# An attention and GEGLU block: last two chunks of 256 queries, Gelu table in the tail, PV in groups of four, LN1 partly on Pool

One core of one Trainium2 chip. The metric is the device time of one execution in microseconds, lower is better. A run is one execution; the first of each kernel is also profiled. PE is TensorE, PEld its weight loads, DVE VectorE, ACT ScalarE, POOL GpSimd, SP SyncE.

## The reference

```
x: [1, 2048, 640]   wqkv: [640, 1920]   wo: [640, 640]     32 heads of 20
w_gate, w_up: [640, 1728]   w_down: [1728, 640]            all bf16, LayerNorm without weights

h  = x + softmax(q k^T * 20**-0.5) v @ wo     with q, k, v = layernorm(x) @ wqkv
out = h + (gelu_tanh(layernorm(h) @ w_gate) * (layernorm(h) @ w_up)) @ w_down
```

## The kernel before

The program lists operations with their reads, writes, PSUM banks and a guessed duration. A small list scheduler, run when the program is built, turns these into one fixed order for each engine.

The queries go in four chunks of 512. In chunk 0 attention shares TensorE with the projections. In the later chunks it shares TensorE with the "post" stage of the chunk before it: output projection, second LayerNorm, gate/up, down. The post stage of the last chunk comes after all attention, with nothing beside it: the tail.

A head has 20 dimensions, so four heads fit in four 32-row groups of the array for QK, and in four 32-column groups for PV. In chunk 0 a unit is two score tiles (two banks), in later chunks three.

```python
tiles = [(c, g, kt, j) for c in range(NC) for g in range(NG) for kt in range(NT) for j in range(4)]
n2 = 64 * NG
units = [tiles[i:i + 2] for i in range(0, n2, 2)] + [tiles[i:i + 3] for i in range(n2, len(tiles), 3)]

def unit(u):
    ...                                                    # (cut: QK matmuls, one group of 2 or 3)
    op("act", I("activation", pts[:, u % 3, 0:n], PS[...], ACT.Exp, scale=SCALE), ...)
    for i, (c, g, kt, j) in enumerate(tl):                 # PV, right after its own exp
        op("pe", I("matmul", PS[32 * j:32 * j + VW, 512 * 6:512 * 7], v_all[:, kt, 4 * g + j, :], pts[...],
                   tile_position=(0, 32 * j), ...), 0.13, P_PV, ...)

for i in range(4):                                         # LN1, four tiles of 128 rows at a time
    for t in range(4 * i, 4 * i + 4):
        ln_stats(x_sb[:, t, :], t, ...)                    # DVE
    ln_rsqrt(4 * i, P_BG)                                  # DVE, 17 small operations on [128, 4]
    for t in range(4 * i, 4 * i + 4):
        ln_apply(x_sb[:, t, :], t, ...)                    # DVE tensor_scalar (x - mu) * rs, 128x640
        transposes(...)                                    # PE, evacuated by ACT

def post(c, banks):                                        # gate/up part of it
    for f in range(NF):                                    # 14 blocks of hidden units
        ...                                                # gate matmuls into a bank
        # DVE: copy, square, multiply-add;  ACT: Tanh;  DVE: multiply-add
        ...                                                # up matmuls
        # DVE: (tanh chain) * 0.5 * up
```

Pool pads the q and k weights in the prologue (12 copies); before that it fills memory with zeros. The post stages beside attention have one PSUM bank, number 7; the tail has all eight.

## Time and profile before

1160.09 us, median of three runs (1157.93 to 1163.11). Stages, read off the timeline of the profiled run (1161.9 us):

| stage | from, to (us) | length | bound by |
|---|---|---|---|
| prologue, to the first exp | 0, 51.1 | 51.1 | DVE queue, then projections |
| chunk 0, to the first 1536-column exp | 51.1, 341.2 | 290.2 | TensorE |
| chunks 1 to 3, to the end of the last exp | 341.2, 1064.5 | 723.3 | ScalarE |
| tail | 1064.5, 1161.9 | 97.4 | DVE in gate/up |

The table of windows of the kernel before at these times. Each line has the stretch, its length, and the busy microseconds of each engine (with its instruction count), then the granted TensorE clock, the share of the DMA engines and GB/s:

```profile
core 0: us, PE busy (x) PEld busy (x) DVE busy (x) ACT busy (x) POOL busy (x), PEclk, DMA share, GB/s
0.00:51.06 51.06, 27.09 (x182) 13.95 (x183) 41.60 (x160) 15.07 (x22) 19.31 (x37) 1.00 0.36 122
51.06:341.23 290.17, 283.98 (x1496) 85.66 (x1495) 122.90 (x228) 246.35 (x256) 0.00 (x0) 1.00 0.00 1
341.23:1064.50 723.27, 639.20 (x4162) 183.09 (x4160) 225.80 (x456) 711.90 (x554) 0.00 (x0) 0.90 0.05 15
1064.50:1161.90 97.40, 66.44 (x339) 32.54 (x339) 62.88 (x130) 8.81 (x15) 0.00 (x0) 0.89 0.03 11
```

Read across each line for the engine that is nearly as busy as the stretch is long. In chunk 0 that is PE (284 of 290), in chunks 1 to 3 ACT (712 of 723), in the tail neither: PE and DVE take turns. A busy PE is not PE at its peak, since matmuls overlap and their ends are modelled; the 639 us of chunks 1 to 3 hold the post stages of chunks 0 to 2 as well.

Two lines of the groups by shape of the kernel before, the only two copies of Pool; the columns are line, engine, operation, names, shapes, count, then busy us and mean ns of one, then idle before it:

```profile
L257 POOL COPY regw<-rege 128x560 bf16<-128x560 bf16 x10 | 6.6, 662 | 0.6
L257 POOL COPY regw<-rege 128x400 bf16<-128x400 bf16 x2 | 1.1, 534 | 0.2
```

Besides these, Pool sets memory and builds two identity masks of 128x128.

The timeline of PE in chunk 0 of the kernel before (start, duration, group, count). The end of a matmul is modelled, so read start to start:

```profile
122.38 0.39 PE L257 MATMUL ps<-qt_all,kt_all 32*128 32x512 bf16 x2
122.70 0.39 PE L257 MATMUL ps<-pts,v_all 128*21 128x512 bf16 x2
123.02 0.45 PE L477 MATMUL ps<-regw 128*128 128x320 bf16 x2
123.40 0.39 PE L257 MATMUL ps<-qt_all,kt_all 32*128 32x512 bf16 x2
```

QK to PV is 0.32 us and PV to the projections is 0.32 us, for two matmuls each. In a later chunk of the same trace, QK to PV is 0.32 us for three:

```profile
440.63 0.39 PE L257 MATMUL ps<-qt_all,kt_all 32*128 32x512 bf16 x3 [0.17 <-ACT pts L257]
440.95 0.39 PE L257 MATMUL ps<-pts,v_all 128*21 128x512 bf16 x3
```

### The profile page before, as it was taken

The numbers are of one execution on the slowest core, as the hardware profiler recorded it, in microseconds if no ns is written. First come the engines' busy times: TensorE is split into PE (matmuls) and PEld (weight loads), VectorE is DVE, ScalarE is ACT, GpSimd is POOL, SyncE is SP. The second block draws the span as 40 slices with busy tenths as digits, with TensorE's granted clock in tenths as the row PEclk, the third lists the DMA queues.
The fourth block names the chain that finished last, engine by engine and source line by source line (L and its number), as shares of the span: only waits on it lengthen the run. The fifth ranks groups of instructions, "written<-read, shape, count | busy, mean of one in ns | idle before, by whom it ended". The sixth has DMA issues, their size and how long they took to land.

```text
span 1161.9 us, 14374 instructions
## 1 busy us (share of the span) xinstructions
PE 1016.7 (88%) x6176; PEld 315.2 (27%) x6176; DVE 453.2 (39%) x973; ACT 982.1 (85%) x846; POOL 19.3 (2%) x37
## 2 busy tenths in 40 slices
PE   2999999999998988988898888998989888888567
PEld 1332332222222222222122222222222222322224
DVE  7733335535634444411024444210143444112783
ACT  1598887797699999999999999999999999996010
POOL 6000000000000000000000000000000000000000
PEclk9999999999999899999567999988598999995899
DMA  5000000000014000000000000000000000000000
GB/s 203 12 1 1 1 1 1 1 1 1 1 69 173 1 1 1 1 12 24 1 12 1 1 1 1 7 6 23 1 12 1 1 1 1 12 18 7 11 0 23
DMA packets 11823, 18.69 MB, mean 16 GB/s; under 512 B 688, under 2 KB 9840, under 8 KB 11760
## 3 DMA queue, kind: packets, MB, share of 16 engines
q1 hardware_dynamic: 11760, 17.78, 4.5%
q8 instruction: 48, 0.79, 0.3%
q14 instruction: 15, 0.12, 0.0%
HBM read 15.16 MB, written 2.62 MB: 15 GB/s over the span
## 4 chain that ended last, share of the span: by engine, by line
ACT 56%; PE 33%; DVE 9%; DMA 1%; issue 1%; SPq 0%; DVEq 0%
ACT pts L257 54%; PE ps L257 18%; PE ps L477 7%; ACT rege L257 2%; PE ps L676 2%; DVE rege L257 2%; PE ps L512 1%; PE ps L643 1%; DVE stats L257 1%; PE ps L443 1%; PE ps L661 1%; DMA rege<-in_A_x_dram 1%; DVE rege L648 1%; PE ps L612 1%; PE ps L588 1%
## 5 line engine op out<-in xcount | busy, mean ns | idle before, releaser
L257 ACT ACTIVATE pts<-ps 128x1536 bf16<-128x1536 f32 (+1 forms) x768 | 951.6, 1474 | 59.5 <-PE ps L257 58.4
L257 PE MATMUL ps<-qt_all,kt_all 32*128 32x512 bf16 x2048 | 318.0, 416 | 81.7 <-ACT pts L257 64.4
L257 PE MATMUL ps<-pts,v_all 128*21 128x512 bf16 x2048 | 324.6, 418 | 0.9 <-ACT pts L257 0.9
L257 PEld LDWEIGHTS ps<-qt_all,kt_all 32*128 32x128 bf16 x2048 | 73.8, 92 | 331.4 <-ACT pts L257 258.4
L477 PE MATMUL ps<-regw 128*128 128x512 bf16 (+1 forms) x480 | 136.6, 359 | 1.9 <-DVE v_all L539 0.6
L257 PEld LDWEIGHTS ps<-pts,v_all 128*21 128x21 bf16 x2048 | 72.7, 89 | 197.6 <-issue 187.6
L257 ACT ACTIVATE rege<-rege 128x512 f32<-128x512 bf16 (+1 forms) x56 | 46.7, 835 | 66.7 <-DVE rege L257 66.7
L661 PE MATMUL ps<-rege,regw 128*128 128x512 bf16 (+1 forms) x280 | 79.3, 388 | 19.6 <-ACT rege L257 17.7
L676 PE MATMUL ps<-regw,rege 128*128 128x320 bf16 x448 | 85.6, 305 | 1.1 <-DVE rege L665 1.0
L643 PE MATMUL ps<-rege,regw 128*128 128x512 bf16 (+1 forms) x280 | 85.4, 401 | 1.1 <-DVE rege L451 0.6
L257 DVE SCALAR_TENSOR_TENSOR rege<-rege 128x512 bf16<-128x512 bf16 (+1 forms) x112 | 76.5, 688 | 17.0 <-ACT rege L257 14.6
L648 DVE CAST rege<-ps 128x512 bf16<-128x512 f32 (+1 forms) x56 | 38.5, 688 | 82.3 <-PE ps L643 82.0
L680 DVE TENSOR_TENSOR rege<-ps,rege 128x320 bf16<-128x320 f32 x32 | 15.7, 491 | 137.5 <-PE ps L676 137.5
L665 DVE SCALAR_TENSOR_TENSOR rege<-rege,ps 128x512 bf16<-128x512 bf16 (+1 forms) x56 | 38.3, 684 | 64.1 <-PE ps L661 64.1
L257 DVE COPY osb<-ps 128x512 f32<-128x512 f32 x32 | 22.1, 690 | 104.1 <-PE ps L257 103.8
L477 PEld LDWEIGHTS ps<-regw 128*128 128x128 bf16 x480 | 40.8, 98 | 69.4 <-issue 48.5
L676 PEld LDWEIGHTS ps<-regw,rege 128*128 128x128 bf16 x448 | 34.9, 97 | 43.1 <-issue 28.6
L443 PE MATMUL ps<-ident,xn_t 128*128 128x128 bf16 x160 | 18.6, 272 | 29.3 <-DVE xn_t L257 29.0
L501 DVE TENSOR_SCALAR kt_all<-ps,e 128x512 bf16<-128x512 f32 x28 | 21.0, 749 | 57.2 <-PE ps L477 57.2
L661 PEld LDWEIGHTS ps<-rege,regw 128*128 128x128 bf16 (+1 forms) x280 | 20.5, 99 | 59.1 <-ACT rege L257 24.6
L504 DVE CAST qt_all<-ps 128x512 bf16<-128x512 f32 x31 | 21.2, 685 | 38.1 <-PE ps L477 38.1
L477 PE MATMUL ps<-wo,rege 128*128 128x320 bf16 x160 | 33.8, 329 | 0.5 <-DVE rege L624 0.4
(57 smaller groups left out, 417.0 us busy)
## 6 DMA issues: line engine op xcount, KB each, us to landing
rege<-in_A_x_dram SPq DMA_DIRECT2D x4, 640.0 KB, 10.1
rege<-in_A_x_dram SPq DMA_DIRECT2D x16, 160.0 KB, 2.2
out_dram<-rege SPq DMA_DIRECT2D x16, 160.0 KB, 1.8
regw<-in_B_w_gate_dram SPq DMA_DIRECT2D x1, 2160.0 KB, 8.2
regw<-in_B_w_up_dram SPq DMA_DIRECT2D x1, 2160.0 KB, 13.2
regw<-in_B_w_down_dram SPq DMA_DIRECT2D x1, 2080.0 KB, 19.5
rege<-in_A_wqkv_dram SPq DMA_DIRECT2D x1, 1600.0 KB, 8.2
regw<-in_A_wqkv_dram SPq DMA_DIRECT2D x1, 800.0 KB, 11.2
```

Of the source, the lines that this page charges most:

```text
L257: return lambda eng: getattr(eng, method)(*args, **kwargs)
L443: op("pe", lambda eng, a=a: eng.transpose(bank16(bk, D)[:, 128 * a:128 * a + 128], src[:, a * 128:(a + 1) * 128], ident[:]), c_mm(128), pr ...
L477: yield op("pe", lambda eng, l=l, r=r, k=k: eng.matmul(bank(bk, n), l, r, start=(k == 0), stop=(k == len(steps) - 1)), c_mm(n), prio, read ...
L501: op("dve", lambda eng: eng.tensor_scalar(dst, bank(bk), e0[:, 0:1], None, ALU.add), c_dve(512), prio, reads=[key, "e0"], writes=[(nm, g, ...
L504: op("dve", lambda eng: eng.tensor_copy(dst, bank(bk)), c_dve(512), prio, reads=[key], writes=[(nm, g, c)], rel=[bk])
L512: op("pe", lambda eng: eng.matmul(bank(b2), gm[:], sq[:, sqi, :], start=True, stop=True), c_mm(512), prio, reads=[("sq", sqi), "gq", "gqh" ...
L643: op("pe", lambda eng, a=a, bg=bg, f=f, m=m: eng.matmul(bank(bg)[0:m, :], wg[:, a, f * 128:f * 128 + m], hnT[:, a, :], start=(a == 0), sto ...
L648: op("dve", lambda eng, bg=bg, g16=g16, m=m: eng.tensor_copy(g16, bank(bg)[0:m, :]), c_dve(512), p, reads=[kg], writes=[("gb", i)], rel=[b ...
L661: op("pe", lambda eng, a=a, bu=bu, f=f, m=m: eng.matmul(bank(bu)[0:m, :], wu[:, a, f * 128:f * 128 + m], hnT[:, a, :], start=(a == 0), sto ...
L665: hdone.append(op("dve", lambda eng, bu=bu, g16=g16, f=f, m=m: eng.scalar_tensor_tensor(out=ha[0:m, f, :], in0=g16, scalar=0.5, in1=bank(b ...
L676: op("pe", lambda eng, f=f, m=m, tt=tt, hf=hf, bk=bk: eng.matmul(bank(bk, 320), ha[0:m, f, tt * 128:(tt + 1) * 128], wd[0:m, f, hf * 320:( ...
L680: op("dve", lambda eng, bk=bk, tt=tt, hf=hf, i=i: eng.tensor_tensor(ob[:, i, hf * 320:(hf + 1) * 320], bank(bk, 320), h_sb[:, tt, hf * 320 ...
```

## The change

Its intent, in five parts: (1) LN1: x is loaded ahead of wqk, rsqrt runs over eight tiles at once with two Newton steps, and ten of the sixteen applications go to Pool. (2) In chunk 0 the PV matmuls of two exps are issued as one group of four. (3) The last 512 queries become two chunks of 256, so that the tail has half the work. (4) In the tail, the Gelu table replaces the tanh chain, and ScalarE evacuates transposes. (5) Scheduler constants, and one shared buffer (hnT) for the transposed attention output.

```diff
-NC = S // 512
+CHUNKS = ((0, 512), (512, 512), (1024, 512), (1536, 256), (1792, 256))
 ...
-            return 0.03 + passes * n / 1900.0
+            return 0.015 + passes * n / 2000.0
 ...
-        load_x(0)
+        for i in range(4):
+            load_x(i)
         load(wqk, ...)
-        load_x(1)
-        load_x(2)
-        load_x(3)
 ...
+        def ln_apply(eng, src, dst, dkey, t, rkeys, prio):
+            return op(eng, I("tensor_scalar", dst, src, mu[:, t:t + 1], rs[:, t:t + 1], ALU.subtract, ALU.mult),
+                      0.7 if eng == "pool" else c_dve(D, 0.5), prio, ...)
 ...
-        for i in range(4):
+        for i in range(2):
+            for t in range(8 * i, 8 * i + 8):
+                ln_stats(...)
+            ln_rsqrt(8 * i, 8, P_BG)
+            for t in range(8 * i, 8 * i + 8):
+                eng = "pool" if t % 8 < 5 else "dve"
+                ln_apply(eng, x_sb[:, t, :], xn_p[:, t % 6, :], ("xnp", t % 6), ...)   # six slots
+                transposes(xn_p[:, t % 6, :], ...)
 ...
+            pv_wait.extend((p0 + i, tl[i]) for i in range(len(tl)))
+            if small and u % 2 == 0:          # chunk 0: PV waits for the second exp
+                return
+            ...                               # then one group of PV matmuls, 0.32
 ...
+                if tail:
+                    ... eng.activation(s16, bank(bg)[0:m, :], ACT.Gelu_apprx_tanh)   # ScalarE
+                else:
+                    ...                       # tanh chain as before
+                if tail:
+                    ... eng.tensor_tensor(fv, s16, bank(bu)[0:m, :], ALU.mult)       # the one DVE operation
 ...
-            post(c, BG1 if c < NC - 1 else ALLB)
+            tail = c == len(CHUNKS) - 1
+            post(c, ALLB if tail else BG1, tail)
```

## The prediction

> **What bounds the kernel now.** The timeline gives five stages. (1) Prologue: first exp at 51 us. (2) Chunk 0, 51 to 342: TensorE busy 49 of every 50 us (table of windows), ScalarE 41: TensorE bounds it. (3) Chunks 1 to 3, 342 to 1064.5, 241 us each: ScalarE bounds them. An exp of 1536 columns comes every 1.344 us: 512 are 688 us, 42 tanh at 0.51 are 21, about 12 are stalls where the granted clock is 0.5 (580-600, 626-636, 825-840, 868-880) and the chain of waits goes over to PE. (4) Tail, 97 us, all exposed: 23 us of output projection and LayerNorm, 54 of gate/up paced by DVE (8.5 of 10 us busy), 17 of down matmuls.
>
> **What changes.**
>
> - Prologue: 10 of 16 LN1 applications go to Pool; two rsqrt chains of 13-15 operations replace four of 17; x loads go ahead of wqk. From the last xn application (42.2 us) to the first exp is 9 us. DVE loses about 12 us of 43, but Pool must first pad the weights (8.4 us, beginning somewhat later). First exp about 42 us: saves 9.
> - Chunk 0: a group of two PV matmuls takes 0.32 us start to start, groups of three in later chunks 0.32 too; so four in one group should. PV costs 41 us instead of 82. Counting the instruction order: before, 164 us attention + 93 other matmuls + 262 returns to attention at about 0.12 = 288 (measured 291). The 0.12 is from the timeline: one 320-column matmul between groups takes 0.27 us instead of 0.14. The Trainium skill (TensorEngine Tiling, Key Properties) says changing the tiling mode drains TensorE; the trace agrees with a gap of that size. After: 123 + 98 + 250 returns = 251, above ScalarE's 256 x 0.92 = 235. Chunk 0 about 254: saves 37.
> - Chunks 1 and 2: ScalarE's work unchanged. 241 each.
> - Last two chunks: ScalarE's work is the same, 171 x 1.344 + 19 x 0.51 = 239. TensorE has twice the attention matmuls at half the width; I estimate 0.32 to 0.36 us a group, hence about 104 us of 120 in each. Chunk 2's down and chunk 3's gate/up slip later; by the order, 41 gate/up and 56 down matmuls of chunk 3 remain after the last QK. With a cold clock at the start, 245 for both: loses 4 against 241.
> - Tail: 8.5 us to finish chunk 3's gate/up (one bank, tanh chain), 13 output projection mixed with chunk 3's down, 7 LayerNorm and transposes, 19 gate/up (140 matmuls of 256 columns at 0.12 plus a cold start), 12 down and store: 60 us. Saves 37. Gelu needs one table load, 1.28 us as in this trace (the skill's ScalarE: Activation LUTs, What ACT_TABLE_LOAD costs, agrees), hidden in LayerNorm; DVE does one operation per 512 columns instead of five.
>
> Sum: 42 + 254 + 482 + 245 + 60 = 1083 us; range 1060 to 1108. Faster by over 2%: 0.97; within: 0.02; slower: 0.01.
>
> **What would show it.** First exp near 42; four-matmul PV groups still 0.32 us from the next; first 1536-column exp near 296; last exp near 1023; exps of the last chunks 1.34 us apart; the tail's gate/up bound by PE, with ScalarE and DVE mostly idle.
>
> **What would make it wrong.** 256-column groups costing 0.4 us or more: the last chunks become TensorE-bound (plus 10 to 20 us). Longer cold-clock stretches. Pool applications over 1 us each, delaying the first exp. A longer serial tail through the one shared bank and hnT, which now also holds the transposed attention output.

## More of the kernel before

The guessed durations decide the order; the chip then runs each queue in that order, whatever the real durations are.

The LayerNorm application that the change moves runs on DVE here, for both LayerNorms, at 0.46 us each:

```profile
L257 DVE TENSOR_SCALAR xn_t<-rege,mu,rs 128x640 bf16<-128x640 bf16 x32 | 13.7, 462 | 0.2
```

## The result

1111.47 us, median of four runs (1107.33 to 1119.48), against 1161.05 us for the kernel before (four runs). The ratio is 0.9584, 95% interval 0.9524 to 0.9643. Here and below a ratio is the mean time of one kernel's runs over that of the other's of the same rounds, so it is not quite the ratio of the medians. Faster, then, but 28 us slower than predicted and 3 us above the range.

The table of windows of the changed kernel, at its own stage limits (profiled run, 1108.0 us):

```profile
core 0: us, PE busy (x) PEld busy (x) DVE busy (x) ACT busy (x) POOL busy (x), PEclk, DMA share, GB/s
0.00:65.37 65.37, 27.95 (x155) 14.92 (x156) 31.19 (x104) 15.24 (x23) 44.44 (x47) 0.90 0.27 96
65.37:316.26 250.89, 247.17 (x1528) 73.50 (x1528) 132.60 (x237) 241.85 (x256) 0.00 (x0) 1.00 0.02 9
316.26:1042.84 726.58, 656.95 (x5326) 207.12 (x5326) 252.72 (x525) 715.61 (x560) 0.00 (x0) 0.86 0.04 13
1042.84:1108.00 65.16, 47.41 (x334) 32.36 (x332) 21.65 (x52) 9.20 (x14) 0.00 (x0) 0.87 0.05 16
```

| stage | before | predicted | after |
|---|---|---|---|
| prologue | 51.1 | 42 | 65.4 |
| chunk 0 | 290.2 | 254 | 250.9 |
| ScalarE-bound chunks | 723.3 | 727 (482 + 245) | 726.6 |
| tail | 97.4 | 60 | 65.2 |
| sum | 1161.9 | 1083 | 1108.0 |

Three stages came within about 5 us. The prologue is off by 23, and in the wrong direction: predicted to gain 9 us, it lost 14. POOL is busy 44.4 us there, against 19.3 before.

The groups by shape of the changed kernel, Pool's costliest and its copies:

```profile
L257 POOL TENSOR_SCALAR rege<-rege,mu,rs 128x640 bf16<-128x640 bf16 x10 | 25.2, 2518 | 5.8 <-DVE rs L257 4.9
...
L257 POOL COPY regw<-rege 128x560 bf16<-128x560 bf16 x10 | 6.6, 661 | 0.6
```

An application takes 2.52 us on Pool; the same operation took 0.46 us on DVE in the trace of before. The scheduler had been told 0.7. The chain of waits of the changed kernel, from 22.9 to 53.7 us, is mostly Pool (start, duration, what; gaps of about 0.1 us marked "issue" are left out):

```profile
22.87 2.51 POOL rege L257
25.46 2.51 POOL rege L257
28.06 2.51 POOL rege L257
30.66 2.51 POOL rege L257
33.26 2.52 POOL rege L257
35.91 0.69 PE ps L441 x5
...
40.03 0.42 DVE sq L257
40.46 0.12 DVE rs L257
40.67 2.68 POOL rege L257
43.44 2.51 POOL rege L257
46.04 2.51 POOL rege L257
48.64 2.50 POOL rege L257
...
65.39 1.01 ACT pts L257
```

What is cut after 35.91 is nine projection matmuls and their evacuation by ScalarE; what is cut at the end is Pool's tenth application, to 53.74, and then 11.6 us of transposes, projections and DVE work. The two groups of five do not join up: Pool waits 4.9 us, until 40.67, for the second rsqrt. DVE's queue, in the fixed order, holds that rsqrt behind work that itself waits for tiles from Pool, directly or through TensorE. The timeline of DVE in the changed kernel:

```profile
19.91 0.43 DVE L257 BATCH_NORM_STATS2 stats<-rege 128x6 f32<-128x320 bf16 x1
26.17 0.45 DVE L257 TENSOR_SCALAR rege<-rege,mu,rs 128x640 bf16<-128x640 bf16 x1 [5.83 <-PE ps L441]
26.54 0.20 DVE L257 BATCH_NORM_AGGREGATE mv<-stats 128x2 f32<-128x12 f32 x1
```

DVE's second application writes one of the six slots, and must wait until Pool's first tile in it has been transposed. It stands 5.83 us still, and the last statistics of the second half stand behind it.

What the prediction said of TensorE can be checked on start-to-start times. PE in chunk 0 of the changed kernel, to be held against the four lines of before:

```profile
98.80 0.39 PE L257 MATMUL ps<-qt_all,kt_all 32*128 32x512 bf16 x2
99.12 0.40 PE L257 MATMUL ps<-pts,v_all 128*21 128x512 bf16 x4
99.44 0.45 PE L478 MATMUL ps<-regw 128*128 128x320 bf16 x2
99.82 0.39 PE L257 MATMUL ps<-qt_all,kt_all 32*128 32x512 bf16 x2
```

Four PV matmuls take 0.32 us, as two did. And PE in a chunk of 256 queries of the changed kernel:

```profile
882.41 0.39 PE L257 MATMUL ps<-qt_all,kt_all 32*128 32x256 bf16 x6
882.73 0.40 PE L257 MATMUL ps<-pts,v_all 128*21 128x256 bf16 x6
```

Six matmuls of 256 columns take 0.32 us from QK to PV, as three of 512 did. The fear of a TensorE-bound end was unfounded.

### The profile page after: what moved, and what is told of

Its sections match the earlier page's. It is cut to its first block, busy times and chain, and to the rows that moved or that the text cites. A ratio compares the mean times of both kernels' runs of the same rounds, so it can differ in the third digit from the quotient of the medians. Undisturbed runs are those within 1.5% of the kernel's fastest.

```text
span 1108.0 us, 16649 instructions
## 1 busy us (share of the span) xinstructions
PE 979.5 (88%) x7340; PEld 327.9 (30%) x7340; DVE 438.2 (40%) x917; ACT 981.9 (89%) x851; POOL 44.4 (4%) x47
## 4 chain that ended last, share of the span: by engine, by line
ACT 55%; PE 37%; DVE 3%; POOL 3%; DMA 1%; issue 0%; POOLq 0%; SPq 0%
ACT pts L257 53%; PE ps L257 17%; PE ps L478 10%; PE ps L678 4%; POOL rege L257 2%; ACT rege L257 2%; PE ps L513 2%; PE ps L722 2%; PE ps L624 1%; PE ps L441 1%; DMA rege<-in_A_wqkv_dram 1%; DVE rege L257 1%; POOL regw L257 1%; DVE rege L693 1%; DVE rege L709 0%
## 5 line engine op out<-in xcount | busy, mean ns | idle before, releaser
L257 PE MATMUL ps<-qt_all,kt_all 32*128 32x512 bf16 (+1 forms) x2560 | 327.7, 374 | 55.7 <-ACT pts L257 53.2
L257 PE MATMUL ps<-pts,v_all 128*21 128x512 bf16 (+1 forms) x2560 | 286.5, 376 | 1.0 <-DVE osb L257 0.9
L678 PE MATMUL ps<-rege,regw 128*128 128x512 bf16 (+2 forms) x700 | 161.8, 350 | 18.8 <-DVE rege L693 6.5
L678 PEld LDWEIGHTS ps<-rege,regw 128*128 128x128 bf16 (+1 forms) x700 | 56.8, 101 | 86.8 <-issue 27.7
L257 DVE COPY osb<-ps 128x512 f32<-128x512 f32 (+1 forms) x40 | 23.3, 582 | 142.9 <-PE ps L257 142.9
L257 DVE SCALAR_TENSOR_TENSOR rege<-rege 128x512 bf16<-128x512 bf16 (+2 forms) x98 | 67.5, 689 | 20.9 <-ACT rege L257 19.3
L257 ACT ACTIVATE rege<-rege 128x512 f32<-128x512 bf16 (+1 forms) x49 | 35.2, 719 | 8.7 <-DVE rege L257 8.5
L624 PE MATMUL ps<-identf,osb 128*128 128x128 f32 x128 | 33.5, 344 | 2.5 <-DVE osb L257 1.3
L524 DVE SCALAR_TENSOR_TENSOR qt_all<-ps,khalf,qt_all 128x512 bf16<-128x512 f32 x32 | 24.0, 750 | 21.1 <-PE ps L513 21.1
L540 DVE CAST v_all<-ps 128x320 bf16<-128x320 f32 x32 | 15.7, 492 | 42.0 <-PE ps L478 42.0
```

What stands on the lines that cost most here:

```text
L257: return lambda eng: getattr(eng, method)(*args, **kwargs)
L524: op("dve", lambda eng: eng.scalar_tensor_tensor(out=dst, in0=bank(b2), scalar=khalf[:, g:g + 1], in1=dst, op0=ALU.add, op1=ALU.add), c_dv ...
L540: op("dve", lambda eng: eng.tensor_copy(dst, src()), c_dve(320), prio, reads=[key], writes=[("v", kt, hf)], rel=[bk])
L624: op("pe", lambda eng, tt=tt: eng.transpose(bank(b2)[:, tt * 128:(tt + 1) * 128], osb[:, s, tt * 128:(tt + 1) * 128], identf[:]), c_mm(128 ...
L678: op("pe", lambda eng, a=a, f=f, fi=fi, mf=mf: eng.matmul(bank(bk)[0:mf, fi * nq:(fi + 1) * nq], w[:, a, f * 128:f * 128 + mf], hnT[:, a, ...
```

## The experiments

Theory A: the miss lies in Pool, at 2.5 us an application, with DVE's queue held behind it. Rival B: loading wqk after all of x delays the padding of the weights, and so everything that Pool does after it. Rival C: the eight-tile rsqrt batches and the six slots serialise the prologue, whatever engine applies. Stage lengths below are read from each kernel's profiled run.

### LN1 on DVE

```diff
-                eng = "pool" if t % 8 < 5 else "dve"
+                eng = "dve"
```

> The changed kernel with all 16 LN1 applications on DVE (0.46 us each), everything else kept, x loads first included. Theory A (the miss lies in Pool: 2.5 us per application, ten of them, and DVE's queue held behind them): first exp at 40 to 44 us instead of 65, every later stage as in the changed kernel (chunk 0 about 249 us, tail about 65 us), total about 1088 us, ratio to the kernel before about 0.938. Rival B (loading wqk after all of x delays the padding and so the first exp): first exp stays above 55 us, total above 1100. Rival C (the eight-tile rsqrt batches and the six xn slots serialise the prologue whatever engine applies): first exp stays above 50 us.

Measured: correct; 1084.11 us median of four runs (1078.57 to 1090.41), ratio to before 0.9377 (0.9326 to 0.9428). First exp at 44.45 us, just outside the 40 to 44 expected; padding still begins at 14.3 us, and the batches and slots are kept. So B and C fall as main causes. The later stages are about as in the changed kernel (721.2 against 726.6, which is inside the spread of profiled runs told below, and 65.6 against 65.2 us). The windows of its prologue and chunk 0:

```profile
0.00:44.45 44.45, 24.75 (x178) 14.06 (x181) 37.37 (x119) 14.73 (x22) 19.24 (x37) 1.00 0.39 141
44.45:290.06 245.61, 238.43 (x1476) 71.30 (x1502) 130.78 (x231) 241.85 (x256) 0.00 (x0) 1.00 0.02 6
```

Chunk 0 became 5 us shorter too (245.6 against 250.9), which theory A did not expect. The instruction order explains a part: with 0.7 us for Pool, the scheduler put 35 V-projection matmuls ahead of the first QK and left 125 for chunk 0; with DVE it put 59 ahead and left 101. An estimate: 24 matmuls of 320 columns at 0.14 us (the step of before's timeline) are about 3 us.

### wqk loaded early again

```diff
-        for i in range(4):
-            load_x(i)
+        load_x(0)
         load(wqk, ...)
+        load_x(1); load_x(2); load_x(3)
```

> The changed kernel with only the load order of the kernel before (x part 0, wqk, then the other x parts); the applications stay on Pool. Theory A: padding starts at 13.7 instead of 14.4 us, Pool applications still 2.5 us each, first exp at 64 to 67 us, total within 3 us of the changed kernel (about 1110). Rival B: first exp falls to about 45 us, total about 1090.

Measured: correct, one run, 1116.93 us, state unknown. Padding starts at 13.63 us and the first exp comes at 64.64. The total is 5 us above the median of the changed kernel but inside its spread (1107 to 1119); it missed the "within 3 us", which a single run cannot carry. The first exp decides: the load order is worth 0.7 us.

### What is slow on Pool

Two kernels with a wrong result on purpose. The order of the queues is unchanged.

```diff
-   tensor_scalar(dst, src, mu[:, t:t+1], rs[:, t:t+1], subtract, mult)
+   tensor_copy(dst, src)                                   # first kernel
+   tensor_scalar(dst, src, 0.0, 20.0, subtract, mult)      # second kernel
```

> Wrong result on purpose: the ten Pool applications are plain copies of the same 128x640 tile; order of all queues unchanged. If the operation itself is what is slow on Pool: a copy takes about 0.75 us (the 128x560 pad copies take 0.66), the ten take 8 us instead of 25, first exp at about 46 to 50 us. If Pool is slow because DVE contends for SBUF, copies beside the same DVE work are slow as well, over 1.5 us.

> Wrong result on purpose: the ten Pool applications keep subtract and multiply but with constants in place of the two per-partition operands. If fetching the per-partition operands is what costs: about 0.8 to 1 us each and first exp at about 48 us. If the two arithmetic operations on Pool cost 2.5 us: no change, first exp at 65 us.

Measured, one run each, state unknown: relative error 0.87 and 0.15, as meant. The timeline of Pool, first with copies:

```profile
22.76 3.89 POOL L257 COPY rege<-rege 128x640 bf16<-128x640 bf16 x5
32.20 3.97 POOL L257 COPY rege<-rege 128x640 bf16<-128x640 bf16 x5 [5.55 <-DVE rs L257]
```

then with constants:

```profile
22.71 12.09 POOL L257 TENSOR_SCALAR rege<-rege 128x640 bf16<-128x640 bf16 x5
40.21 12.07 POOL L257 TENSOR_SCALAR rege<-rege 128x640 bf16<-128x640 bf16 x5 [5.42 <-DVE rs L257]
```

Five copies take 3.9 us, 0.78 each with the gap to the next (0.74 without), and the first exp comes at 45.65 us (total 1094.96). Five subtract-and-multiply with constants take 12.1 us, 2.4 each, and the first exp stays at 63.65 us (total 1108.69). So the arithmetic is what costs; the per-partition operands add only about 0.2 us. Contention with DVE is not it: copies beside the same DVE queue are fast, and in the changed kernel an application at 48.64 us, in an 11 us stretch where DVE does nothing, took 2.50 us as the others did. What was not run is the same ten applications with 2.5 us told to the scheduler, so how much of the loss better ordering could win back is open.

The copy kernel keeps the order and the length of chunk 0 of the changed kernel (250.8 us) although its prologue is 20 us shorter. So that 5 us of chunk 0 goes with the order which the scheduler chose, not with the late start.

### One part at a time, on the kernel before

First the PV groups alone, in chunk 0:

```diff
-  PV of each exp after it, two operations of one matmul
+  PV of two exps after the second, one operation of four matmuls; pts with four slots of two tiles
```

> The kernel before with the PV of two exps issued as one group in chunk 0 and nothing else. If a group of four PV matmuls takes the same 0.32 us as a group of two: chunk 0 falls from 291 to about 252 us, prologue and chunks 1 to 3 and tail unchanged, total about 1121 us, ratio about 0.966. Rival: if a group of four takes about twice a group of two, or if chunk 0 got shorter in the changed kernel only because more projections were done in the longer prologue: chunk 0 stays above 275 us, ratio above 0.985.

Measured: correct; 1123.88 us (1122.87 to 1128.52), ratio 0.9684 (0.9648 to 0.9721). Chunk 0 took 254.6 us, the tail 97.5 as before. The group of four costs what a group of two costs; this part alone is worth 36 to 39 us.

Then the LN1 part alone (loads, rsqrt over eight tiles, ten applications on Pool):

> The kernel before with the LN1 part of the change alone (x loads first, two eight-tile rsqrt chains of two steps, ten applications on Pool). Pool theory: first exp moves from 51 to about 65 us, so this part alone costs about 12 to 14 us less whatever projection work the idle TensorE can do earlier (little): total about 1173 us, ratio about 1.011. If instead the LN1 part was a gain in isolation: ratio below 1.0.

Measured: correct; 1180.77 us (1179.23 to 1182.89), ratio 1.0171 (1.0130 to 1.0211), which a verdict at 2% calls unclear but which lies above 1. The first exp comes at 62.2 us, 11 later than before, and chunk 0 takes 300.0 us, 10 longer: the scheduler left 144 V-projection matmuls in chunk 0 instead of 107. The loss is larger than I expected, because I had not counted that second part. The LN1 part is a loss in itself.

### What the split and the Gelu table are worth

Both start from the kernel with LN1 on DVE. First the split undone:

```diff
-CHUNKS = (..., (1024, 512), (1536, 256), (1792, 256))
+CHUNKS = (..., (1024, 512), (1536, 512))
```

> The changed kernel with LN1 on DVE and the last two chunks of 256 put back to one of 512 queries; Gelu table and ScalarE evacuations of the tail kept. By sum: gate/up 280 matmuls of 512 columns at 0.216 is 30 us for 512 queries, bound by PE; tail about 75 us against 65, chunks before it 241 us as ever, total about 10 us over the kernel with LN1 on DVE, about 1094. If the split is what gives the tail most of its gain: tail about 95 us, total 1112 or more.

Then the Gelu table and ScalarE evacuations undone:

```diff
-            post(c, ALLB if tail else BG1, tail)
+            post(c, ALLB if tail else BG1, False)
```

> The changed kernel with LN1 on DVE and the split kept, but the last post stage with the old tanh chain and DVE evacuations. By sum: seven gate/up steps at 3.6 us (the pace in the tail of the kernel before) are 25 to 27 us instead of 19, evacuations 1 us more: tail about 73 us, total about 8 us over the kernel with LN1 on DVE, about 1092. If the Gelu table gives the tail most of its gain: tail over 85 us.

Measured, both correct: without the split 1091.6 us (1090.63 to 1098.63), ratio 0.9412 (0.9370 to 0.9453); without the table 1097.91 us (1097.11 to 1099.73), ratio 0.9455 (0.9424 to 0.9486). Their tails in the table of windows, first without the split, then without the table:

```profile
1021.81:1096.80 74.99, 62.69 (x336) 33.19 (x339) 26.18 (x63) 14.69 (x23) 0.00 (x0) 0.89 0.04 14
```

```profile
1018.83:1095.50 76.67, 49.10 (x334) 31.70 (x332) 40.02 (x84) 5.54 (x9) 0.00 (x0) 0.87 0.04 13
```

The tail is 97.4 us with neither, 75.0 with the table alone, 76.7 with the split alone, 65.6 with both. Either part takes about 21 us by itself, and the second adds only 9 to 11: both attack the same 54 us of gate/up (1087.8 to 1142.1 in the trace of before). (The expectation's "280 matmuls of 512 columns" should read 140: the trace of before has 140 in the tail, and 140 at 0.216 are its 30 us.) With the table, PE is busy 62.7 of 75 us, so its matmuls bound the tail; with the tanh chain on half the queries PE and DVE take turns. These are tails of one trace each. In total time the split is worth less: the ratio without it is 0.9412, with it 0.9377 and in a second set 0.9363 (below), some 4 to 6 us, and the intervals overlap. Without the table it is 0.9455, some 10 us more.

Part 5 of the change was not run alone. An estimate from the ratios and tails: 37 for the PV groups and 32 for the tail, less 20 for the LN1 part, is 49 us; the whole change gained 48 by its ratio, so little is left for it.

### The cold clock at the ends of chunks

Before each chunk's end, the post stage of the previous chunk is done and only attention runs. The granted clock then falls to 0.5 (0.51 from 550 to 600 us in the kernel before), and the next post stage begins at that clock; exps then wait for PE. The fillers are matmuls whose result nothing reads, at the lowest priority, after each of the first two post stages:

```diff
+            if c in (0, 1):
+                dn = (len(sc.ops) - 1,)
+                for _ in range(70):               # second kernel: (96, 94)[c]
+                    fb = Bank(7)
+                    op("pe", lambda eng, fb=fb: eng.matmul(bank(fb), ident[:], kt_all[:, 0, 0:512], start=True, stop=True),
+                       c_mm(512), 9, reads=[...], acq=[fb], rel=[fb], after=dn)
```

> The kernel with LN1 on DVE plus 70 filler matmuls (128x512, result unused, into bank 7) after each of the first two post stages, in the stretches where only attention runs and the granted clock is 0.5. If those cold stretches cost the 10 to 15 us of stalls in the ScalarE-bound stage: the clock stays at 1.0 through the ends of chunks 1 and 2, the stage from the first 1536-column exp to the last exp falls from 721 (one run; 721 to 733 in others) to about 714, total falls by 5 to 12 us against the same kernel without fillers, with less spread. Rival: the stalls come from the order of the projection and LayerNorm work at the start of a post stage, not from the clock: the stage stays at 720 or more and the total equals the kernel without fillers within 3 us.

> The kernel with LN1 on DVE again, as the partner of the run with fillers on the same chip: ratio to the kernel before 0.933 to 0.943, total 1078 to 1090 us, stage from the first 1536-column exp to the last exp 720 to 733 us.

> As the run with 70 fillers, but 96 and 94 of them, so that they go on across the ends of chunks 1 and 2 instead of ending some 7 us before[...]. If the cold clock at the chunk ends makes the stalls: granted clock near 1.0 across both ends, the stage from the first 1536-column exp to the last exp at 712 to 718 us instead of 721 to 733, total 1072 to 1080 us, ratio about 0.927. Rival (the order of the work at a chunk's end makes the stalls): stage still above 720, ratio 0.933 or more, as with 70 fillers.

Measured, all correct, six runs each, of which five in timed rounds: with 70 fillers 1083.22 us (1081.96 to 1091.19), ratio 0.9334 (0.9321 to 0.9348); without fillers 1086.25 (1080.24 to 1091.52), ratio 0.9363 (0.9334 to 0.9392); with 96 and 94 fillers 1077.28 (1074.22 to 1079.34), ratio 0.9284 (0.9268 to 0.9300).

The 70 fillers kept the clock up while they lasted, but the last ones ended at 522.2 and 764.1 us, 9 and 11 us before the last exp of the chunk, and the clock was at 0.5 again when the post stage began. By the terms of its expectation this run went the rival's way: the stage took 733.5 us, not 714 (in the slowest of its six runs, which was the profiled one), and the total is within 3 us of the kernel without fillers. Since the clock fell before the chunk end, it decides nothing. The longer set speaks for the clock at two chunk ends, in one trace. The table of windows over those two ends, without fillers:

```profile
530.00:600.00 70.00, 63.53 (x438) 20.85 (x439) 34.83 (x79) 69.36 (x56) 0.00 (x0) 0.89 0.02 6
770.00:830.00 60.00, 54.01 (x608) 19.16 (x609) 26.97 (x71) 57.48 (x45) 0.00 (x0) 0.86 0.03 7
```

with 70 fillers:

```profile
530.00:600.00 70.00, 65.37 (x398) 20.38 (x398) 30.95 (x72) 64.42 (x50) 0.00 (x0) 0.75 0.02 6
770.00:830.00 60.00, 55.16 (x554) 18.61 (x553) 23.73 (x65) 55.85 (x43) 0.00 (x0) 0.71 0.02 7
```

with 96 and 94:

```profile
530.00:600.00 70.00, 62.37 (x454) 20.63 (x458) 34.85 (x79) 70.00 (x57) 0.00 (x0) 1.00 0.02 6
770.00:830.00 60.00, 52.11 (x645) 19.21 (x647) 29.05 (x74) 60.00 (x48) 0.00 (x0) 1.00 0.03 7
```

The fourth busy number is ACT: 70.00 of 70 and 60.00 of 60 at clock 1.00, against 69.36 and 57.48 at 0.89 and 0.86 without fillers, and 64.42 and 55.85 at 0.75 and 0.71 with 70. In these three traces the idle time of ScalarE goes with the clock. Two parts of the expectation missed. The stage from the first 1536-column exp to the last took 721.0 us in the profiled run, not 712 to 718, and "above 720" was the rival's mark. At the end of chunk 0, which has no fillers, the clock was cold in that run (0.68 from 290 to 340 us, where ScalarE idles 5.2 us; 0.77 and 3.0 us without fillers). The two profiled runs without fillers had 721.2 and 723.0, and each was the fastest run of its set. So the traces show the stalls gone at two ends, worth 3 us against the traced run without fillers, but not the gain of the whole. That gain rests on the timed runs: the ratio of 0.9284 lies a little above the 0.927, but its interval lies clear of the kernel without fillers. The two were not timed side by side: the longer set ran later on the same chip, against the runs of the kernel before from the earlier session, with one new run of it (1159.04 us) in line with those. This version is the fastest: 82 us below before, 34 below the change as it came. It also spreads less, 5 us over six runs instead of 11.

## Why the prediction was wrong

Point by point, in the order of the prediction:

- **Prologue, "First exp about 42 us: saves 9".** This is the step that failed. The sum took away DVE's work and delayed Pool's start, but held no term for ten applications on Pool; the list of risks named "over 1 us each" without a number behind it. Measured: 2.52 us each, 25.2 in all, on the chain from 22.9 us on, with a gap of 5 us in the middle because DVE's queue stood behind Pool. The prediction's 42 us, less the 9 us that it takes from the last application to the first exp, puts the last application at 33; Pool's tenth ended at 53.74, 21 us later, and the first exp followed 11.6 us after it, at 65.4. With the applications on DVE it came at 44.45, and the time was 1084 to 1086 us, against the 1083 predicted. That the total then agrees so well is partly luck: in the first of these traces the prologue is 2.5 us over its term, chunk 0 8 under, the ScalarE stage 6 under and the tail 6 over.
- **Chunk 0, "PV costs 41 us instead of 82".** Right. Four matmuls take 0.32 us; chunk 0 took 250.9 us against 254; alone, the part gave 254.6. The 0.12 us at each return to attention, which I put beside the drain that the Trainium skill describes (TensorEngine Tiling, Key Properties), carried the sum within 3 us. Read off both traces it is nearer 0.10 us (between PV and the next QK, one projection matmul of 0.14 us takes 0.24 from start to start, two take 0.38), and just as long where the last exp had ended over 0.15 us before, so it is not a wait for an exp. That it is a drain was not tested.
- **Chunks 1 and 2, last two chunks.** Right: 726.6 us against 727, and the groups of 256 columns took 0.32 us. That it is right to 1 us is luck: in the profiled runs of the five-chunk variants this stage took 721 to 733.5 us.
- **Tail, 60 us.** Right in mechanism, 5 us short. The finish of chunk 3's gate/up took 10.6 us instead of 8.5 (1042.8 to 1053.4). LayerNorm took about 10.5 instead of 7 (1066.8 to 1077.3); 2.4 us of it is DVE waiting at 1070.05 for the residual x, whose load waits for an output store from the same buffer. Gate/up took 18.6 against 19. The table load took 1.28 us, as the skill gives for the load itself (ScalarE: Activation LUTs, What ACT_TABLE_LOAD costs), and ran beside the first gate matmuls, not in LayerNorm. The page adds about 1.38 us of drain; here ScalarE had just ended its evacuations 0.02 us before, and after the load it waited for PE, so no run shows such a drain.
- **Cold clock.** I had put the stalls of before down to it from the trace. The longer fillers support it at two chunk ends, in one trace; the gain in time is shown by the timed runs. The Trainium skill (TensorE: Matmul & The Clock Gate, Part 1, What's actually happening) says that the clock is throttled by default and that activity releases it, by windows of about 3.4 us; here it fell 5.7 and 2.7 us after the end of the last of the 70 fillers (at 527.9 and 766.8 us).

The net of the terms: prologue +23, chunk 0 -3, ScalarE stage 0, tail +5, together the 25 us between 1083 and the profiled 1108. Nothing is left over that needs another cause, apart from the run-to-run spread of 12 us.

## What to carry to other kernels

Before work moves to an engine, price that operation on that engine: a copy's time on it says nothing of arithmetic, and if no trace has the operation, the sum has a hole that a range of 2% will not cover. A wrong duration in a static scheduler costs twice, once for the slow operation, and again because other queues are ordered around a time that never comes. Two remedies for one bottleneck do not add: the table and the split took 22 and 21 us off the tail alone, but 32 together.

## What the Trainium skill lacked or had wrong

- GPSIMD Engine Reference, Engine selection: it calls one-input elementwise work on GPSIMD roughly line-rate, and two-input work about twice slower than VectorE. A bf16 tensor_scalar with subtract and multiply, one tensor input of 128x640, took 2.52 us on Pool against 0.46 us on DVE, 5.5 times; with constants 2.4 us. Only the plain copy, 0.74 us, comes near what the page says.
- TensorE: Matmul & The Clock Gate: it lets the ratio follow how busy PE has been, and speaks of idle gaps as what brings the slow clock back. Here attention alone, in 32-row and 32-column tiles, with PE busy 8.5 of every 10 us by the profile (560 to 570 us in the kernel before), ran at a granted 0.50; up to two full 128x512 matmuls more in each 1.34 us, as the 70 fillers were, held it at 1.00 (473.3 to 528 us, in the run with 70 fillers). I found no statement there of what such tiled matmuls count for as activity.
- TensorEngine Tiling, Key Properties: it says that changing the tiling mode drains the engine, and gives no figure. About 0.12 us at each return to attention fitted chunk 0 within 3 us, in two kernels (288 for 290 before, 251 for 251 after); read from start to start it is 0.10. Whether it is that drain no run here shows.
